# A two-layer attention and long-convolution kernel: the convolution's buffers laid out anew, its inverse table loaded later, the second attention's first weights placed low

## The chip, the cores and the metric

The kernel runs as one program on one core of a Trainium2 chip. The metric is device time in microseconds (us). Before the change three runs took 2643.77, 2644.64 and 2650.95 us; the median is 2644.64 us. One more execution was recorded by the hardware profiler.

The core has a tensor engine (PE, whose weight loads are listed as PEld), a vector engine (DVE), a scalar engine (ACT), GpSimd (POOL) and SyncE (SP), which here only issues DMAs. Each engine works through its own list of instructions in order; an instruction that waits holds up all those behind it on that engine.

## The reference

The input is x of 2048 rows and 640 columns. Two kinds of layer alternate, each twice:

```python
x = x + A(layernorm(x))      # 32-head softmax attention, head size 20, with wqkv and wo
x = x + B(layernorm(x))      # long convolution along the rows, one filter per column
x = x + A(layernorm(x))
x = x + B(layernorm(x))

# A: q, k, v = (x @ wqkv) split in heads; softmax(q k^T / sqrt(20)) v; @ wo
# B: K = 2 * real(sum_n C[d,n] * exp(A[d,n] * dt[d] * l))     # a filter of 2048 taps per column
#    y = irfft(rfft(u, 4096) * rfft(K, 4096), 4096)[:2048] + u * D_skip
```

Everything is float32 at the interface; both A layers share their weights, and both B layers share K, so the filter's spectrum is worked out once.

## The kernel before

The program runs through: first attention (0 to about 1085 us, in which the filter K is also worked out beside the softmax), the first output projection together with the filter's spectrum (to about 1260), the first convolution (to about 1404), the head of the second attention (to about 1469: layer norm, transposes and the projections of the first block of heads), its main part (to about 2447, where ACT computes exponentials nearly without a gap), the second output projection (to about 2498) and the second convolution (to the end).

**Convolution.** Columns are worked in five blocks `b` of 128. `stage1(b, x1, i2)` is the first step of the transform: eight groups `i2`, each a set of 12 matmuls into a PSUM tile `psx` (two such tiles exist), an ACT cast `x10<-psx` to f16 and a DVE subtraction `x11<-psx,x10` for the rest. `stage2a` transposes that (`pst`, copied to `xt` by ACT), `sets(xt)` makes the second step (48 matmuls into `psx`). `product` multiplies with the filter's spectrum: DVE `t<-psx` and `ka<-psx,ka`, then POOL `kb<-t,kb` and `ka<-ka,kb`. `stage3` and `stage4` go back (`psv` with `fa`, then `psy` with the inverse table `eb`, 2048 KB), and DVE adds `psy` to x. These steps are staggered over a loop `n`: step `n` has the transposes of column part `n`, the product of part `n-4`, and `psy` from `n = 14` on.

The spectrum lies in DRAM in `kha` and `khb`, one tensor each, stored by ten pairs of DMAs (`kha<-kn`, `khb<-kn`). `factors` loads one piece of 256 KB of each per step; there are five buffers `ka` and three `kb`, so a load `kb` is issued when POOL has used the one three steps earlier. `eb` is loaded whole before the first `stage1`, in memory that overlaps the tiles `u` and `kn` of the stage before.

**Second attention's head.** `stage(...)` loads a weight and returns a function that later splits it in f16 halves: ACT casts (`wb`, in the trace `wb<-b0s`), DVE subtracts (`wb<-b0s,wb`), and in the second attention a DVE maximum `wm<-b0s` looks for the largest weight. `b0s` and `b1s` (320 KB each) hold the first q and k weights. They lie in memory that overlaps `eb`, so that they are loaded after the last `psy` of the first convolution. Four row groups `i4` are normalised (`bn_stats`, `va`, `lt`, `rs`, `nb`, then ACT `xn`), transposed (`pst`), split in `xh` (ACT) and `xl` (DVE), and multiplied (`pq`, `pv`).

The order on each engine comes from the order of the code, changed by a scheduler: an instruction goes onto its engine's list when the scheduler's model finds its inputs and its memory free, so a buffer's address also sets the place in the list.

In the listing below, line numbers are those of the profile. A helper issues most DVE, ACT and DMA instructions and is L78 in all rows; matmuls of the convolution are L1430, its transposes L1452, POOL's products L1480; the transposes of attention's head are L823, its `pq` L773.

Of the kernel before, what the change touches and what calls it, by code (L numbers as in the profile page):

```python
# [21 lines left out]
P = 128  # L22
# [4 lines left out]
H = 32  # L27
# [60 lines left out]
def mha_s4d_kernel(ctx, tc, x_in, wqkv, wo, lar, aim, cr, ci, ldt, dsk,  # L88
# [26 lines left out]
    kd = dram.tile([D, L], F32, name="kd")  # L115
    dtd = dram.tile([1, D], F32, name="dtd")
    wd = dram.tile([P, 3, len(LV), D], F32, name="wd")
    kha = dram.tile([2 * NCT, P, 4, 4, P], F32, name="kha")
    khb = dram.tile([2 * NCT, P, 4, 4, P], F32, name="khb")
    qs = dram.tile([2, D, L], F16, name="qs")  # L120
    ks = dram.tile([2, D, L], F16, name="ks")
    qm = dram.tile([H, L], F16, name="qm")
# [309 lines left out]
    def attention(x, stats):  # L432
# [50 lines left out]
        def stage(c0, n, tag, dst=None, pool=None):  # L483

            full = QW if pool or tag == "v" else P
            ts = tag + "s" if pool else "ws"
            wt = (pool or q2).tile([P, NCT, QW], F32, tag=ts, bufs=1, name=ts)[:, :, :n]
            cols = c0 if isinstance(c0, tuple) else (c0,)
            m = n // len(cols)
            for k, c_ in enumerate(cols):  # L490
                sy.dma_start(wt[:, :, k * m:k * m + m], wqkv[:, c_:c_ + m].rearrange("(t p) c -> p t c", p=P))

            def make():
                bufs = 1 if tag == "v" else 2
                wh, wl = dst or [q2.tile([P, NCT, full], F16, tag=tag + t, bufs=bufs, name=tag + t)[:, :, :n]
                                 for t in "hl"]
                if not first_layer:
                    ve.reduce_max(wm[:, made[0]:made[0] + 1], wt, axis=AX.XY,
                                  apply_absolute_value=True)
                made[0] += 1  # L500
                if pool:
                    se.activation(wh, wt, AF.Copy, scale=WS)
                else:
                    ve.tensor_scalar_mul(wh, wt, WS)
                ve.scalar_tensor_tensor(wl, wt, WS, wh, ALU.mult, ALU.subtract)
                return wh, wl
            return make
        made = [0]

        def post(w_, b, tq, qc, pool=None):  # L510

# [245 lines left out]
        with ExitStack() as c2:  # L757
            psum(c2, M=2, S=4)
            hp = c2.enter_context(tc.tile_pool(name="hp", bufs=1))
            xp = c2.enter_context(tc.tile_pool(name="xnp", bufs=2))  # L760
            self_ = hp.tile([P, NBLK * H], F32, name="self")
            NQ = 3 if first_layer else 1
            wv = [hp.tile([P, NCT, NQ * QW], F16, name=f"wv{n}") for n in range(2)]
            wb = [[hp.tile([P, NCT, P], F16, name=f"wb{w_}{n}") for n in range(2)] for w_ in range(2)]
            last[0] = None

            def block0(tq):
# [23 lines left out]
                return ts  # L791

            coming = load_x(0)
            made_ = [stage(n * D, P, f"b{n}", wb[n], hp) for n in range(2)]
            if first_layer:
                filler[:2] = kgen(), False
                weave(1)
            sy.dma_start(self_, c_sel)
            for i4 in range(4):
                xr = coming  # L800
                if i4 < 3:
                    coming = load_x(i4 + 1)
                if stats is None:
                    mv, rs = ln_stats(lambda i: xr[i], 4)
                else:
                    mv, rs = stats(i4)
                xn = []
# [12 lines left out]
                for ct in range(NCT):  # L820
                    pt = pst("S", [P, 512], F32, tag="S", name="pst")
                    for i in range(4):
                        te.transpose(pt[:, i * P:i * P + P], xn[i][:, ct * P:ct * P + P], ident)  # L823
                    sl = slice(512 * i4, 512 * i4 + 512)
                    se.copy(xh[:, ct, sl], pt)
                    ve.tensor_sub(xl[:, ct, sl], pt, xh[:, ct, sl])
                block0(i4)
                if i4 == 0:
                    for make in made_:
                        make()  # L830
                    nxt.append(stage((P, D + P), 64, "w"))
                else:
                    values4(i4 - 1)
# [561 lines left out]
    def ssm(x, uh, ul, consts, last):  # L1395
        st = None
        if not last:
# [4 lines left out]
            mv = sp_.tile([P, NI, 2], F32, name="mv5")  # L1402
            done = {}

            def final(i4):

                if i4 not in done:
                    s4 = slice(4 * i4, 4 * i4 + 4)
                    for i in range(4 * i4, 4 * i4 + 4):
                        ve.bn_stats(st[:, i, NCT - 1, :], x[:, i, (NCT - 1) * P:])  # L1410
                        ve.bn_aggr(mv[:, i, :], st[:, i, :, :])
                    done[i4] = mv[:, s4, :], rstd(mv[:, s4, :], 4, sp_, f"rs{i4}")
                return done[i4]
        e1, f2, id16, fa = consts
        with ExitStack() as c:
            c1 = c.enter_context(tc.tile_pool(name="s1", bufs=1))
            if last:
                cx = c.enter_context(tc.tile_pool(name="sx", bufs=2))
            c4 = c.enter_context(tc.tile_pool(name="s4", bufs=1))
            c2 = c.enter_context(tc.tile_pool(name="s2", bufs=2))  # L1420
            c3 = c.enter_context(tc.tile_pool(name="s3", bufs=3))
            if not last:
                cx = c2
            order = {}

            def at(name, made):
# [1 line left out]

            def mm(*a, **k):
                at("pe", te.matmul(*a, **k))  # L1430
            eb = c1.tile([P, NI, 2, P], F32, name="eb")
            sy.dma_start(eb, c_eb.rearrange("p (i r k) -> p i r k", i=NI, r=2))

            def stage1(b, x1, i2):
                bs = slice(b * P, b * P + P)
# [78 lines left out]
            def new_x1():  # L1514
                return [cx.tile([P, 4, NI // 2, 4, 32], F16, name=f"x1{k}") for k in range(2)]

            x1 = new_x1()
            for i2 in range(8):
                stage1(0, x1, i2)()
            ks, t1s, vs = {}, {}, {}  # L1520
            NQ = 8 * NCT
            nxt, px = None, None
            sums = None
            for n in range(NQ + 15):
# [3 lines left out]
                if n < NQ:  # L1528
                    if q == 0 and b:
                        x1 = nxt  # L1530
                    if n % 4 == 0:
                        xt = c4.tile([P, 2, 4, 4, P], F16, name="xt")
                    stage2a(x1, q, xt)
                if 2 <= n < NQ + 2:
                    ks[n - 2] = factors(*divmod(n - 2, 4))
                if sums:
                    sums[0]()
                if 4 <= n < NQ + 4:
# [7 lines left out]
                    sums = None  # L1546
                if 6 <= n < NQ + 6:
                    m, ch = divmod(n - 6, 4)
                    if m % 2 == 0 and ch == 0:
                        vs[m // 2] = c2.tile([P, 2, NI, 4, 32], F32, name="v")  # L1550
                    stage3(vs[m // 2], m % 2, ch, t1s.pop(n - 6))
                if 14 <= n < NQ + 14:
                    bb, i2 = divmod(n - 14, 8)
# [240 lines left out]
```

## Time and profile before

| quantity | value |
|---|---|
| runs | 2643.77, 2644.64, 2650.95 us (median 2644.64) |
| profiled execution: span from the first to the last instruction | 2647.0 us |
| busy in that span: PE, PEld, DVE, ACT, POOL | 2492.4, 1409.8, 1519.5, 2344.0, 801.7 us |
| mean granted TensorE clock | 0.994 of full speed |
| chain of work that ended last: ACT, PE, issue, DVE, DMA, POOL | 59, 20, 10, 3, 2, 1 % |

Busy shares are over the whole span, and the stages have different limits: in the main part of both attentions ACT is busy nearly throughout, in the convolutions PE and POOL share the load. What a change in one stage is worth has to be read in that stage: which engine ends last there, and what released it. The profiled execution's span is the only time that the profile has for it; it is 2.4 us above the median of the runs.

### The profile page before, as it was taken

The numbers are of one execution on the slowest core, as the hardware profiler recorded it, in microseconds if no ns is written. First come the engines' busy times: TensorE is split into PE (matmuls) and PEld (weight loads), VectorE is DVE, ScalarE is ACT, GpSimd is POOL, SyncE is SP. The second block draws the span as 40 slices with busy tenths as digits, with TensorE's granted clock in tenths as the row PEclk, the third lists the DMA queues.
The fourth block names the chain that finished last, engine by engine and source line by source line (L and its number), as shares of the span: only waits on it lengthen the run. The fifth ranks groups of instructions, "written<-read, shape, count | busy, mean of one in ns | idle before, by whom it ended". The sixth has DMA issues, their size and how long they took to land.

```text
span 2647.0 us, 118800 instructions
## 1 busy us (share of the span) xinstructions
PE 2492.4 (94%) x52388; PEld 1409.8 (53%) x52388; DVE 1519.5 (57%) x3430; ACT 2344.0 (89%) x2763; POOL 801.7 (30%) x1230
## 2 busy tenths in 40 slices
PE   6899999999999999899898999999999998999898
PEld 3444444454444444587896544454444443444898
DVE  7587777777765887577786323232232222143875
ACT  7899999999999999655665899999999999999574
POOL 1123333233323332111681122222222223222285
PEclk9999999999999999999999999999999999999999
DMA  6522222322222221654652111121121113222466
GB/s 206 189 53 77 68 74 62 82 65 63 61 54 59 53 63 38 234 206 163 213 173 64 47 53 50 51 60 45 45 66 39 50 34 87 71 66 61 137 190 184
DMA packets 188158, 241.99 MB, mean 91 GB/s; under 512 B 43504, under 2 KB 128816, under 8 KB 186224
## 3 DMA queue, kind: packets, MB, share of 16 engines
q1 hardware_dynamic: 151936, 188.28, 22.6%
q0 software_dynamic: 35696, 46.01, 7.4%
q8 instruction: 413, 6.77, 1.1%
q14 instruction: 113, 0.93, 0.1%
HBM read 158.16 MB, written 76.00 MB: 88 GB/s over the span
## 4 chain that ended last, share of the span: by engine, by line
ACT 59%; PE 20%; issue 10%; DVE 3%; DMA 2%; POOL 1%; SPq 0%; ACTq 0%; POOLq 0%; DVEq 0%
ACT pt L78 57%; PE psy L1430 3%; PE pa L903 2%; PE psv L1430 2%; PE po L193 2%; PE psx L1430 2%; PE S L868 2%; PE pst L1452 1%; PE pkx L193 1%; PE pv L586 1%; PE m L620 1%; PE pkt L196 1%; PE pq L773 1%; DMA kb<-khb 1%; DMA kop<-ks 1%
## 5 line engine op out<-in xcount | busy, mean ns | idle before, releaser
L78 ACT ACTIVATE pt<-S 128x1024 f32<-128x1024 f32 x2048 | 1927.7, 1033 | 27.9 <-PE S L868 15.5
L903 PE MATMUL pa<-pt,V 64*32 64x512 f32 x16384 | 1096.9, 589 | 1.4 <-DVE oc L78 1.4
L868 PE MATMUL S<-qop,kop 61*32 61x512 f16 x16384 | 877.2, 380 | 82.7 <-ACT pt L78 67.8
L868 PEld LDWEIGHTS <-kop 61*32 61x32 f16 x16384 | 366.9, 89 | 737.3 <-issue 619.2
L903 PEld LDWEIGHTS pa<-pt,V 64*32 64x32 f32 x16384 | 312.7, 106 | 72.0 <-issue 8.6
L78 POOL DMA_DIRECT2D dn<-oc x248 | 122.7, 501 | 574.2 <-DVE oc L78 574.1
L78 DVE TENSOR_SCALAR qc<-m 128x512 f32<-128x512 f32 (+1 forms) x68 | 46.8, 688 | 312.0 <-PE m L620 312.0
L78 POOL DMA_DIRECT2D db<-dn x248 | 125.4, 512 | 141.5 <-DMA dn<-dr 136.9
L78 POOL DMA_DIRECT2D ot<-oc x256 | 130.5, 517 | 88.4 <-DVE oc L78 55.5
L620 PE MATMUL m<-xl,wh 64*32 64x512 f16 x2560 | 143.8, 376 | 0.3 <-issue 0.3
L620 PE MATMUL m<-xh,wh 64*32 64x512 f16 x2560 | 144.1, 378 | 0.0
L620 PE MATMUL m<-xh,wl 64*32 64x512 f16 x2560 | 143.8, 377 | 0.0
L78 DVE COPY oc<-pa 128x512 f32<-128x512 f32 x64 | 44.2, 690 | 172.9 <-PE pa L903 168.9
L78 ACT COPY xt<-pst 128x1024 f16<-128x1024 f16 x80 | 81.3, 1016 | 60.8 <-PE pst L1452 60.8
L620 PEld LDWEIGHTS <-wh 64*32 64x32 f16 x5120 | 90.3, 93 | 73.3 <-issue 30.8
L78 POOL DMA_DIRECT2D dn<-dr x62 | 34.6, 558 | 287.3 <-DVE dr L78 248.6
L1480 POOL TENSOR_TENSOR kb<-t,kb 128x512 f32<-128x512 f32 x76 | 97.2, 1280 | 65.2 <-DVE t L78 40.8
L78 DVE TENSOR_SCALAR V<-m 128x160 f32<-128x160 f32 x64 | 20.7, 324 | 163.4 <-PE m L586 163.4
L78 DVE TENSOR_TENSOR kb<-ktab 128x512 f32<-128x512 f32 x160 | 106.2, 683 | 0.0
L586 PEld LDWEIGHTS <-xh 128*128 128x128 f16 x960 | 79.7, 98 | 46.7 <-issue 31.4
L1480 POOL TENSOR_TENSOR ka<-ka,kb 128x512 f32<-128x512 f32 x76 | 97.5, 1283 | 6.0
L337 PEld LDWEIGHTS m<-kb,ka 128*32 128x32 f32 x3840 | 60.8, 109 | 71.0 <-issue 52.4
(312 smaller groups left out, 3936.4 us busy)
## 6 DMA issues: line engine op xcount, KB each, us to landing
ka<-kha SPq DMA_DIRECT2D x80, 256.0 KB
kb<-khb SPq DMA_DIRECT2D x80, 256.0 KB
db<-dn POOLq DMA_DIRECT2D x248, 64.0 KB, 3.2
kop<-ks SPq DMA_DIRECT2D x176, 80.0 KB
kpw<-wd POOLq DMA_DIRECT2D x60, 192.0 KB, 3.9
qop<-qs SPq DMA_DIRECT2D x256, 40.0 KB
ot<-oc POOLq DMA_DIRECT2D x256, 40.0 KB, 3.0
kha<-kn SPq DMA_DIRECT2D x20, 512.0 KB
```

What stands on the lines that cost most here:

```text
L78: made = f(out, *a, **k)
L193: chain(te.matmul(*a, **k))
L196: chain(te.transpose(*a, **k))
L337: chain(te.matmul(ps[32 * j:32 * j + 32, c8, :], a[n][:, ch, :], b[n][:, dd, :], start=(n == 0), stop=(n == 2), tile_position=(0, 32 * j)))
L586: chain(te.matmul(ps[:, :n], a_[:, ct, sl], m[:, ct, :], start=(k == 0), stop=(k == 14)))
L620: chain(te.matmul(ps[r][32 * t:32 * t + 32, :], a_[rows, ct, 32 * u:32 * u + 32], m[rows, ct, 512 * v:512 * v + 512], start=(k == 0), stop ...
L773: te.matmul(pq, a_[:, ct, :], m[:, ct, sl], start=(n == 0), stop=(n == 14))
L868: chain(te.matmul(S[32 * t:32 * t + 32, 512 * r:512 * r + 512], kt_[rows, kc + 32 * t:kc + 32 * t + 32], qt[rows, :], start=True, stop=Tru ...
L903: chain(te.matmul(pa[r][32 * j:32 * j + 32, :], V[rows, kt, VP * h:VP * h + 32], pts[j // 2][rows, 512 * (j % 2):512 * (j % 2) + 512], sta ...
L1430: at("pe", te.matmul(*a, **k))
L1452: at("pe", te.transpose(pt[:, k, g, :], of_group(x1[k], 4 * q + g), id16))
L1480: at("pool", getattr(ge, f)(*a))
```

## The change

1. `kha` and `khb` become ten DRAM tiles each. A load waits for the stores of its own tile and not for all of them, and the first loads are issued before the last store.
2. The convolution's memory pools are laid out anew. The two buffers `v` become `va` and `vb` in separate pools. `eb` shares a pool with `va`, is allocated and loaded at step `n = 6`, behind the loads of part 4; the factors of parts 0 to 2 are issued ahead of `stage1`. `x1` (the tiles of `x10`, `x11`) lies at 72416 to 105184 of the second convolution's memory, where it lay at 51936 to 84704.
3. In the attention's head the tiles of `b0s`, `b1s` are allocated first, so they lie at 65440 to 71840 (before 74528 to 80928), below the memory of `eb`. The looks for the largest value of these two are put off until the last `xl` of row group 0, and so are the statistics of row groups 2 and 3.

```diff
-    kha = dram.tile([2 * NCT, P, 4, 4, P], F32, name="kha")
-    khb = dram.tile([2 * NCT, P, 4, 4, P], F32, name="khb")
+    kha, khb = ([dram.tile([P, 4, 4, P], F32, name=f"kh{t}{m}") for m in range(2 * NCT)] for t in "ab")
...
-                    ve.reduce_max(wm[:, made[0]:made[0] + 1], wt, axis=AX.XY,
-                                  apply_absolute_value=True)
+                    look = lambda n=made[0]: ve.reduce_max(wm[:, n:n + 1], wt, axis=AX.XY, apply_absolute_value=True)
+                    looks.append(look) if made[0] < 2 else look()
...
-            self_ = hp.tile([P, NBLK * H], F32, name="self")
-            wv = [hp.tile([P, NCT, NQ * QW], F16, name=f"wv{n}") for n in range(2)]
-            wb = [[hp.tile([P, NCT, P], F16, name=f"wb{w_}{n}") for n in range(2)] for w_ in range(2)]
...
+            wb = [[], []]
             made_ = [stage(n * D, P, f"b{n}", wb[n], hp) for n in range(2)]
+            for w_ in range(2):
+                wb[w_].extend(hp.tile([P, NCT, P], F16, name=f"wb{w_}{n}") for n in range(2))
...
-                    mv, rs = stats(i4)
+                    mv, rs = stats(i4, turned if i4 > 1 else None)
...
+                if i4 == 0:
+                    turned = xl_.ins
+                    for look in looks:
+                        tie(look(), turned)
...
-                        ve.bn_stats(st[:, i, NCT - 1, :], x[:, i, (NCT - 1) * P:])
+                        tie(ve.bn_stats(st[:, i, NCT - 1, :], x[:, i, (NCT - 1) * P:]), after)
...
+            c0, c4 = (c.enter_context(tc.tile_pool(name=n, bufs=1)) for n in ("s0v", "s4"))
+            cx = c.enter_context(tc.tile_pool(name="sx", bufs=2))
+            c3 = c.enter_context(tc.tile_pool(name="s3", bufs=3))
             c1 = c.enter_context(tc.tile_pool(name="s1", bufs=1))
-            if last:
-                cx = c.enter_context(tc.tile_pool(name="sx", bufs=2))
-            c4 = c.enter_context(tc.tile_pool(name="s4", bufs=1))
-            c2 = c.enter_context(tc.tile_pool(name="s2", bufs=2))
-            c3 = c.enter_context(tc.tile_pool(name="s3", bufs=3))
-            if not last:
-                cx = c2
...
-            eb = c1.tile([P, NI, 2, P], F32, name="eb")
-            sy.dma_start(eb, c_eb.rearrange("p (i r k) -> p i r k", i=NI, r=2))
...
+            ks = {k: factors(*divmod(k, 4)) for k in range(3)}
...
-                if 2 <= n < NQ + 2:
+                if 5 <= n < NQ + 2:
                     ks[n - 2] = factors(*divmod(n - 2, 4))
+                if n == 6:
+                    vs[0] = c1.tile([P, 2, NI, 4, 32], F32, name="va")
+                    eb = c1.tile([P, NI, 2, P], F32, name="eb")
+                    at("sp", sy.dma_start(eb, c_eb.rearrange("p (i r k) -> p i r k", i=NI, r=2)))
```

The first place is SP at the start of the first convolution. Before, `eb` stands behind the last store and ahead of every load; `ka`, `kb` are loads of the spectrum, in order of the part.

```order
734 L78 DMA khb<-kn_28866 128x1024
735 L78 DMA khb<-kn_28870 128x1024
736 L78 DMA eb<-in_c_eb 128x4096
737 L78 DMA ka<-kha 128x512
738 L78 DMA kb<-khb 128x512
739 L78 DMA ka<-kha 128x512
```

In the changed kernel the same stretch of SP reads as follows; `kha_66` is the first of the ten tiles, `kha_67` the second.

```order
735 L78 DMA ka<-kha_66 128x512
736 L78 DMA khb_85<-kn_28888 128x1024
737 L78 DMA kb<-khb_76 128x512
...
744 L78 DMA ka<-kha_67 128x512
745 L78 DMA kb<-khb_77 128x512
746 L78 DMA eb<-in_c_eb 128x4096
747 L78 DMA ka<-kha_67 128x512
748 L78 DMA kb<-khb_77 128x512
```

`eb` has moved behind five pairs of loads (parts 0 to 4) and stands ahead of the loads of part 5. The second convolution has the same order.

The second place is ACT at the start of the second convolution: `x<-psx` are the casts of `stage1`, `oh<-otl`, `u` and `uhx` belong to the second output projection. Before:

```order
431 L78 CAST oh<-otl 128x640
432 L78 CAST x_55485<-psx_55487 128x4x4x32
433 L78 CAST oh<-otl 128x640
434 L78 CAST x_55485<-psx_55502 128x4x4x32
435 L78 ACT_TABLE_LOAD
...
457 L78 CAST uhx<-u 128x640
458 L78 CAST x_55485<-psx_55517 128x4x4x32
459 L78 ACTIVATE lt<-va 128x1
460 L78 CAST x_55485<-psx_55532 128x4x4x32
```

In the changed kernel, where the numbers after `x_` and `psx_` are only names of buffers:

```order
432 L78 CAST oh<-otl 128x640 x2
433 L78 ACT_TABLE_LOAD
...
453 L78 CAST uhx<-u 128x640
454 L78 CAST x_55517<-psx_55519 128x4x4x32
455 L78 CAST x_55517<-psx_55534 128x4x4x32
456 L78 ACTIVATE lt<-va 128x1
457 L78 CAST x_55517<-psx_55549 128x4x4x32
458 L78 CAST x_55517<-psx_55564 128x4x4x32
459 L78 CAST x_55517<-psx_55579 128x4x4x32
460 L78 ACTIVATE u<-x,nb,rs 128x640
```

The first two of the eight casts have moved from the beginning of the output projection to its end, behind the last `uhx` but one. DVE's first two subtractions have moved with them.

The third place is DVE at the end of the first convolution and the start of the second attention's head. Before, the weights stand behind all the statistics:

```order
2235 L78 BN_AGGR mv_28890<-st_28889 128x2 x2
2236 L78 TENSOR_REDUCE wm<-b0s 128x1
2237 L78 TENSOR_SCALAR va<-mv_28890 128x4
2238 L78 TENSOR_REDUCE wm<-b1s 128x1
2239 L78 SCALAR_TENSOR_TENSOR wb_31480<-b0s,wb_31479 128x640
2240 L78 SCALAR_TENSOR_TENSOR wb_31482<-b1s,wb_31481 128x640
2241 L78 CAST sel<-self 128x192
2242 L78 TENSOR_TENSOR xl<-pst,xh 128x512 x5
2243 L78 TENSOR_REDUCE wm<-b0s 128x1
```

In the changed kernel:

```order
2199 L78 SCALAR_TENSOR_TENSOR wb_31503<-b0s,wb_31502 128x640
2200 L78 TENSOR_TENSOR x<-x,psy 128x2x128
2201 L78 RECIPROCAL rs<-lt 128x4
2202 L78 TENSOR_TENSOR x<-x,psy 128x2x128
2203 L78 TENSOR_TENSOR lt<-rs 128x4
2204 L78 SCALAR_TENSOR_TENSOR wb_31505<-b1s,wb_31504 128x640
...
2228 L78 TENSOR_TENSOR xl<-pst,xh 128x512 x5
2229 L78 TENSOR_REDUCE wm<-b0s 128x1
2230 L78 TENSOR_REDUCE wm<-b1s 128x1
2231 L78 SCALAR_TENSOR_TENSOR nb<-mv_28908,rs 128x4
```

The two `wb` subtractions stand among the last additions of `psy`, the two looks `wm` behind the five `xl`. On ACT the casts `wb<-b0s`, `wb<-b1s` have moved in the same way, ahead of the first `lt` and of the four `xn`; on SP the loads of `b0s` and `b1s` wait for the first of the last nine groups of `psy` where they waited for the last.

## Rows read from the trace of the kernel before

**Rows 1.** The page's first line: span and instructions.

```profile
span 2647.0 us, 118800 instructions
```

**Rows 2.** Busy time by stretch: us, PE, PEld, DVE, ACT, POOL, clock, DMA share, GB/s.

```profile
1260.00:1404.00 144.00, 134.22 (x1900) 126.69 (x1897) 113.11 (x303) 87.35 (x166) 102.00 (x90) 0.99 0.54 172
2498.00:2647.00 149.00, 133.72 (x1872) 126.22 (x1871) 98.64 (x213) 86.41 (x162) 98.14 (x77) 0.97 0.63 187
```

**Rows 3.** Chain of work that ended last, first convolution's start: start us, us, what.

```profile
1260.73 4.64 DMA khb<-kn
...
1267.82 8.42 DMA kb<-khb
```

**Rows 4.** Timeline of ACT and PE there; in brackets idle time before, and its releaser.

```profile
1275.16 1.01 ACT L78 COPY xt<-pst 128x1024 f16<-128x1024 f16 x1 [0.25 <-PE pst L1452]
1276.23 0.91 PE L1430 MATMUL psx<-xt,f2s 32*32 32x512 f16 x48 [0.43 <-DMA kb<-khb]
```

**Rows 5.** Timeline of SP's DMA issues: the loads kb of parts 4 and 5.

```profile
1283.58 0.32 SPq L78 DMA_DIRECT2D kb<-khb  x1
...
1286.15 0.32 SPq L78 DMA_DIRECT2D kb<-khb  x1
```

**Rows 6.** Busy time by stretch while eb and the first loads move (columns as above).

```profile
1274.00:1278.00 4.00, 3.09 (x83) 2.67 (x83) 2.23 (x6) 2.53 (x5) 0.00 (x0) 1.00 0.96 351
```

**Rows 7.** Chain at part 5's load, and POOL's addition that takes it.

```profile
1286.15 5.19 DMA kb<-khb
...
1291.48 1.30 POOL L1480 TENSOR_TENSOR kb<-t,kb 128x512 f32<-128x512 f32 x1
```

**Rows 8.** Second convolution's stage1: casts as a group, then timeline of ACT, PE, DVE.

```profile
L78 ACT CAST x<-psx x8: 567/580/587, 2460.7 to 2505.3; 128x512 f16<-128x512 f32 x8
...
2498.55 0.58 ACT L78 CAST x<-psx 128x512 f16<-128x512 f32 x1
2499.91 0.27 PE L1430 MATMUL psx<-uhx,e1s 128*128 128x128 f16 x1 [4.91 <-DVE x L78]
2503.92 0.83 DVE L78 TENSOR_TENSOR ulx<-u,uhx 128x640 f16<-128x640 f32 x1
2505.28 0.59 ACT L78 CAST x<-psx 128x512 f16<-128x512 f32 x1 [0.47 <-PE psx L1430]
```

**Rows 9.** First convolution's last psy on PE, and SP's issue of b0s.

```profile
1395.35 8.43 PE L1430 MATMUL psy<-v,eb 128*128 128x128 f32 x72
1403.81 0.38 SPq L78 DMA_DIRECT2D b0s<-in_wqkv  x1
```

**Rows 10.** Timeline of ACT in the second attention's head.

```profile
1400.30 0.20 ACT L78 ACTIVATE lt<-va 128x4 f32<-128x4 f32 x1 [4.10 <-DVE va L78]
...
1403.95 3.36 ACT L78 ACTIVATE xn<-x,nb,rs 128x640 f32<-128x640 f32 x4 [0.27 <-PE psy L1430]
...
1409.06 2.03 ACT L78 CAST xh<-pst 128x512 f16<-128x512 f32 x4
```

**Rows 11.** Timeline of DVE in the second attention's head.

```profile
1407.29 0.82 DVE L78 TENSOR_REDUCE wm<-b0s 128x1 f32<-128x640 f32 x1 [0.46 <-DMA b0s<-in_wqkv]
1408.42 0.82 DVE L78 TENSOR_REDUCE wm<-b1s 128x1 f32<-128x640 f32 x1 [0.23 <-DMA b1s<-in_wqkv]
1409.15 0.81 DVE L78 SCALAR_TENSOR_TENSOR wb<-b0s,wb 128x640 f16<-128x640 f32 x1
...
1410.79 3.13 DVE L78 TENSOR_TENSOR xl<-pst,xh 128x512 f16<-128x512 f32 x5
```

**Rows 12.** PE's fifth transpose group there, its clock, and pq on the chain.

```profile
1411.53 0.66 PE L823 MATMUL pst<-ident,xn 128*128 128x128 f32 x4 [3.51 <-DVE xl L78]
1412.00:1414.00 2.00, 2.00 (x8) 0.67 (x7) 2.00 (x5) 1.64 (x3) 0.00 (x0) 0.60 0.45 142
1412.18 8.26 PE pq L773 x30
...
1436.94 6.47 PE pq L773 x30
```

More of the change, by code (lines that the diff above doesn't have):

```diff
@@ L507, in stage @@
             return make
-        made = [0]
+        made, looks = [0], []
         def post(w_, b, tq, qc, pool=None):
@@ L793, in attention @@
             coming = load_x(0)
+            wb = [[], []]
             made_ = [stage(n * D, P, f"b{n}", wb[n], hp) for n in range(2)]
+            for w_ in range(2):
+                wb[w_].extend(hp.tile([P, NCT, P], F16, name=f"wb{w_}{n}") for n in range(2))
+            self_ = hp.tile([P, NBLK * H], F32, name="self")
+            wv = [hp.tile([P, NCT, NQ * QW], F16, name=f"wv{n}") for n in range(2)]
             if first_layer:
@@ L825, in attention @@
                     se.copy(xh[:, ct, sl], pt)
-                    ve.tensor_sub(xl[:, ct, sl], pt, xh[:, ct, sl])
+                    xl_ = ve.tensor_sub(xl[:, ct, sl], pt, xh[:, ct, sl])
+                if i4 == 0:
+                    turned = xl_.ins
+                    for look in looks:
+                        tie(look(), turned)
                 block0(i4)
@@ L1403, in ssm, with final @@
             done = {}
-            def final(i4):
+            def final(i4, after=None):
                 if i4 not in done:
@@ L1515, in new_x1 @@
                 return [cx.tile([P, 4, NI // 2, 4, 32], F16, name=f"x1{k}") for k in range(2)]
+            NQ = 8 * NCT
+            t1s, vs = {}, {}
+            ks = {k: factors(*divmod(k, 4)) for k in range(3)}
             x1 = new_x1()
@@ L1519, in ssm @@
                 stage1(0, x1, i2)()
-            ks, t1s, vs = {}, {}, {}
-            NQ = 8 * NCT
             nxt, px = None, None
@@ L1531, in ssm @@
                     if n % 4 == 0:
-                        xt = c4.tile([P, 2, 4, 4, P], F16, name="xt")
+                        xt = c0.tile([P, 2, 4, 4, P], F16, name="xt")
                     stage2a(x1, q, xt)
-                if 2 <= n < NQ + 2:
+                if 5 <= n < NQ + 2:
                     ks[n - 2] = factors(*divmod(n - 2, 4))
+                if n == 6:
+                    vs[0] = c1.tile([P, 2, NI, 4, 32], F32, name="va")
+                    eb = c1.tile([P, NI, 2, P], F32, name="eb")
+                    at("sp", sy.dma_start(eb, c_eb.rearrange("p (i r k) -> p i r k", i=NI, r=2)))
                 if sums:
@@ L1548, in ssm @@
                     m, ch = divmod(n - 6, 4)
-                    if m % 2 == 0 and ch == 0:
-                        vs[m // 2] = c2.tile([P, 2, NI, 4, 32], F32, name="v")
+                    if m % 2 == 0 and ch == 0 and m:
+                        pool, name = ((c1, "va"), (c0, "vb"))[m // 2 % 2]
+                        vs[m // 2] = pool.tile([P, 2, NI, 4, 32], F32, name=name)
                     stage3(vs[m // 2], m % 2, ch, t1s.pop(n - 6))
```

## The prediction

> **What bounds the kernel now.** I read the page's first line first [rows 1], then the busy time by stretch, since the change touches only two convolutions and the 65 us between the first of them and the second attention's softmax. In both convolutions PE is busy 93 and 90% of the stretch and POOL 71 and 66% [rows 2]: neither is idle enough for DMA to be the general limit, so I looked at each end of them for the wait that is last. The chain of waits names two DMA pieces at the first convolution's start, a store of 4.64 us and a load of 8.42 us [rows 3]. The reader is to test these against the timeline: the first `sets` matmul starts at 1276.23, the ACT copy `xt` that it reads ends at 1275.16 + 1.01 = 1276.17 [rows 4]. It follows the copy by 0.06 us. The load that the chain names landed at the same moment, and POOL needs it only two us later. So that start is bound by the transform's own steps, and a DMA that ends earlier changes nothing there.
>
> **The change, part by part.** All times are against the profiled span of 2647.0 us, which lies 2.4 us above the median of the runs; I add the sum to the median.
>
> *Ten tiles, and loads ahead of the last store.* They remove the 4.64 us store and the 2048 KB of `eb` from in front of the first loads. By the paragraph above this is worth nothing: the cover is `stage1`, the transposes and `xt`, which end at 1276.17 anyway. Bounds: a gain of 0.43 us (PE's idle time that the row puts down to the load [rows 4]) and 0. I take 0.
>
> *`eb` late.* It is issued right behind the load `kb` of part 4, so at about 1283.58 + 0.4 = 1284.0 [rows 5], in front of `ka` and `kb` of part 5. Without it, `kb` of part 5 was issued at 1286.15 and landed 5.19 us later at 1291.34, and POOL's addition began at 1291.48 [rows 7]: there is 0.1 us of slack. With it, SP's queue holds at 1284.0 the rest of `kb` of part 4 (up to 0.26 MB), `eb` (2.10 MB) and the two loads of part 5 (0.52 MB), 2.6 to 2.9 MB. At the 351 GB/s that the same transfers reached with the DMA engines 96% busy [rows 6] this is 7.5 to 8.2 us, until 1291.5 to 1292.2; the way from the last byte to the start of the waiting instruction comes on top, and I allow up to 2 us for it. So part 5 lands 0.1 to 2.9 us late; I take 1.5, the middle, as no row is nearer to one end. DVE's multiplication by `ka` waits too, and behind it on DVE the subtractions `x` of `stage1`, which PE waits for. POOL runs without a gap there, so a lost us is not won back. If the transfer is slower than that, the price goes up to the whole transfer, 2.10 MB / 351 GB/s = 6.0 us. Part 6 has two steps more and catches up. The second convolution has the same order and the same pace, so again 1.5. Together +3.0, between 0.2 and 5.8.
>
> The Trainium skill ("DMA: Bandwidth & Descriptors", section "Queues, rings and completion order") says that all DMAs issued by SP share one row of rings and that each ring's descriptors are consumed in order; by that rule a small load behind `eb` waits for nearly all of it, which is what the sum assumes. If the queue let the small loads pass, this term would be near 0 and the sum 3.0 lower. The trace before has no large transfer ahead of a needed load, so no row shows which.
>
> *`stage1` of the second convolution.* Before, the first cast runs at 2460.7, in the output projection, and only six of the eight are left at 2498.55 [rows 8]. Now `x10`, `x11` lie where the second attention's tiles and the projection's `otl` lay, and all eight casts stand behind `uhx` at 2498.55. PE had also worked ahead by two groups; its next `psx` (group 4) waited 4.91 us for DVE to free a tile and started at 2499.91 [rows 8]. Now the same matmul slot does group 2. Two steps more at the pace of the rows, (2505.28 - 2499.91) / 4 = 1.3 us from group 4's matmuls to group 7's cast, are 2.7 us. A check from another side: the last `u` now stands behind the cast of group 4, which comes two steps later, so `u`, `uhx` and DVE's `ulx` (2503.92, 0.83 [rows 8]), which group 7 needs, are later by about the same. After that nothing differs, so the delay goes to the end. Bounds: 0.6 + 0.6 for two casts alone at the row's 0.58, and 3.6 with a late `ulx`. I take +2.8. What the output projection wins by the two casts that leave it is nothing, because PE's projection matmuls run without them.
>
> *The second attention's head.* Before, `b0s` was issued at 1403.81, after the last of nine `psy` groups [rows 9], and landed by 1407.29; `b1s` by 1408.42 [rows 11]. Two looks and two subtractions follow on DVE, 4 x 0.82 less overlap, and `xl` starts at 1410.79; PE's fifth transpose group waits 3.51 us for it [rows 11, 12]. Now the issue waits for the first of the nine, 1395.35 + 8.43 / 9 = 1396.3, so the weights land about 7.5 us earlier, near 1399.8 and 1400.9. The looks leave the path. But the casts of both weights now stand ahead of `lt` on ACT: `lt` ran at 1400.30 [rows 10], now it waits for `b1s` and a cast, about 1401.65, so 1.35 later. From there to `xn` DVE has two subtractions `wb` more (0.81 each [rows 11]) and a few statistics less; `xn` also loses its wait of 0.27 for the last `psy`. I put `xn` at 1404.75, 0.8 late. The last `xn` ends 3.36 later, at 1408.1, its transposes at 1408.8, `xh` starts at 1408.9 (before 1409.06 [rows 10], where it stood behind the casts), and `xl` 0.6 later at 1409.5 instead of 1410.79. So PE's wait ends 1.3 us earlier. Against this, `wv`, whose load needs the buffer of `b0s`, now waits for a look that comes after `xl`, and group 1's `nb` stands behind both looks: some of it comes back, 0.3. I take -1.0. Bounds: -5.3, if all 3.51 us of PE's wait go and PE keeps its clock. Its clock was granted 0.60 in 1412 to 1414, after that wait, and the first `pq` pair took 8.26 us where the next took 6.47 [rows 12], 1.79 more. The other bound is +1, if the late `wv` holds PE.
>
> Sum: 0 + 3.0 + 2.8 - 1.0 = +4.8 us. On the median that is 2644.64 + 4.8 = 2649.4 us; the profiled span would be about 2651.8.
>
> **Rivals.**
>
> *Late loads wait for the whole table (slower).* Place: SP's queue at part 5 of both convolutions. Price: not 1.5 but 6.0 each, if `eb` holds the queue alone and parts 5 and 6 both miss their step. For it: 0.1 us of slack, and POOL without a gap. Against it: at 351 GB/s the queue would be empty by 1292.2. Time: 2644.64 + 12.0 + 2.8 - 1.0 = 2658.4. It decides the sign beyond 0.3% when each stall is over 3.1.
>
> *The head gives all that it can.* The full 5.3. For it: the looks, 1.6 us, were on the path without need. Against it: `lt` behind the casts. Time: 2644.64 + 3.0 + 2.8 - 5.3 = 2645.1.
>
> *The chain is right about the first convolution's start (faster).* If the first products did wait for store and loads, 4.64 us and 6.0 us of `eb` go: 2649.4 - 10.6 = 2638.8; with half of the head's gain 2636.6. For it: the two pieces of the chain [rows 3]. Against it: `xt` ends 0.06 us before the matmul [rows 4].
>
> **How the numbers follow.** A run can tell no change from a change only beyond about 0.3%, 7.9 us: faster is below 2636.7, slower above 2652.6. The forecast has a chance of 0.52, with its own range of 2645.5 to 2653; the table's whole wait 0.16; the head's full gain 0.20; the chain's reading 0.12. Half of the chain's case would be below 2636.7, and a little of the head's: faster 0.08. Slower is nearly all of the first rival and a tenth of the forecast: 0.20. Same is 0.72. The range that leaves 2 in 10 out is 2640 to 2656.
>
> **What would show it.** In the trace after: `eb` issued near 1284 in the first convolution, and a gap on POOL before the addition of part 5, put down to DMA, 0 to 3 us, and one like it in the second. All eight casts of the second `stage1` behind 2498, and the first `xt` some 2.8 us later after the output projection's end than before. `b0s` issued seven us before the last `psy` ends, `lt` behind two casts, PE's wait before the fifth transpose group near 2 us. I am wrong if the first `sets` matmul starts earlier relative to the last spectrum store by more than 1 us, if POOL shows no gap at part 5, or if the time is below 2640.

## The result, and the profile after

The changed kernel takes 2658.69 us (median of 6 runs, 2657.26 to 2662.37); the kernel before, on the same chip, 2648.05 (6 runs, 2643.77 to 2652.91). The ratio is 1.0049, interval 1.004 to 1.0059, which is 13.0 us (10.6 to 15.6): slower by 0.4 to 0.6%. The medians differ by 10.6 us, the lower end of that. The forecast was 2649.4, with a range up to 2656. The first rival, "late loads wait for the whole table", gave 2658.4.

The page's first line, which answers to [rows 1]:

```profile
span 2656.9 us, 118785 instructions
```

Runs of one kernel scatter by some us, and part of that arises before the changed stages, so I compare stretches inside the two profiled runs. Each begins and ends with the start of an instruction that both traces show; the last ends with the span.

| stretch | before | after | difference | forecast |
|---|---|---|---|---|
| program start to the first `sets` matmul | 1276.2 | 1272.8 | -3.5 | 0 |
| first `sets` to first `psy` of the first convolution | 28.2 | 34.7 | +6.5 | +1.5 |
| first `psy` to the second attention's first exponential | 164.8 | 162.6 | -2.2 | -1.0 |
| first to last exponential | 979.5 | 979.4 | -0.1 | 0 |
| last exponential to POOL's first product of the second convolution | 66.3 | 69.4 | +3.1 | +2.8 |
| that product to the end | 131.9 | 138.0 | +6.1 | +1.5 |

The four stretches of the change give +13.5 us, from one profiled execution of each kernel; that lies inside the ratio's interval (0.0049 x 2648 = 13.0), above the difference of the medians. The -3.5 of the first is scatter: it was there some 1150 us earlier, at the first attention's first exponential (114.4 after, 117.8 before).

**First convolution.** The timeline of PE, then of SP, POOL and DVE, and one piece of the chain of waits (start us, us, what; in brackets idle time before, and its releaser). They answer to [rows 4, 5, 7].

```profile
1272.76 0.91 PE L1431 MATMUL psx<-xt,f2s 32*32 32x512 f16 x48 [0.43 <-ACT xt L78]
...
1293.60 0.27 PE L1431 MATMUL psx<-uh,e1s 128*128 128x128 f16 x1 [4.79 <-DVE x L78]
...
1307.49 1.06 PE L1431 MATMUL psy<-va,eb 128*128 128x128 f32 x8
```

```profile
1280.11 0.32 SPq L78 DMA_DIRECT2D kb<-khb  x1
1280.47 0.43 SPq L78 DMA_DIRECT2D eb<-in_c_eb  x1
1280.95 0.43 SPq L78 DMA_DIRECT2D ka<-kha  x1
```

```profile
1286.73 1.27 POOL L1479 TENSOR_TENSOR kb<-t,kb 128x512 f32<-128x512 f32 x1 [1.49 <-DMA kb<-khb]
...
1293.06 1.26 POOL L1479 TENSOR_TENSOR kb<-t,kb 128x512 f32<-128x512 f32 x1 [3.69 <-DVE ka L78]
```

```profile
1292.26 0.69 DVE L78 TENSOR_TENSOR ka<-psx,ka 128x512 f32<-128x512 f32 x1 [3.42 <-DMA ka<-kha]
```

```profile
1280.95 11.29 DMA ka<-kha
```

The load `ka` of part 5, issued right behind `eb`, takes 11.29 us where `kb` of part 5 took 5.19 before [rows 7]; the load that comes last is now `ka`. DVE stands 3.42 us for it, POOL behind DVE 3.69. The load `kb` of part 4, issued 0.36 us before `eb`, is late too, by 1.49. POOL's two gaps are 5.2 us together, and PE's next `psx` stands 4.79 us for DVE's `x`, which comes behind that `ka`. The view by stretch (columns as in [rows 2]) shows the transfer, and what the wait did to PE:

```profile
1280.00:1284.00 4.00, 3.31 (x76) 2.66 (x76) 2.68 (x8) 1.87 (x4) 3.84 (x5) 1.00 0.88 207
1284.00:1288.00 4.00, 3.73 (x50) 3.61 (x49) 1.93 (x3) 3.65 (x6) 2.51 (x2) 1.00 0.94 379
1288.00:1292.00 4.00, 0.81 (x11) 0.69 (x11) 0.79 (x2) 1.56 (x3) 1.29 (x2) 0.96 0.94 352
1292.00:1296.00 4.00, 2.40 (x17) 2.40 (x17) 2.90 (x6) 0.58 (x1) 2.86 (x3) 0.50 0.48 176
```

In 1280 to 1292 the DMA engines moved 4 x (0.207 + 0.379 + 0.352) = 3.75 MB. PE, busy for 0.81 of the four us to 1292, then works at a granted clock of 0.50, the 1.2 GHz level, to 1296 and on to 1298. That is the likely rest between the 5.2 us of the gaps and the 6.5 of the stretch, though no run isolates it: POOL has two more gaps there, this one of 0.66 us and one of 0.21 three us later, put down to DVE's `t`, which reads PE's `psx`.

```profile
1301.51 1.27 POOL L1479 TENSOR_TENSOR kb<-t,kb 128x512 f32<-128x512 f32 x1 [0.66 <-DVE t L78]
```

**Second convolution.** POOL at parts 4 and 5 there: the same two gaps, 4.6 us together.

```profile
2530.42 1.27 POOL L1479 TENSOR_TENSOR kb<-t,kb 128x512 f32<-128x512 f32 x1 [0.92 <-DMA kb<-khb]
...
2536.72 1.26 POOL L1479 TENSOR_TENSOR kb<-t,kb 128x512 f32<-128x512 f32 x1 [3.66 <-DVE ka L78]
```

Its `stage1` on ACT, which answers to [rows 8]: first two casts, last cast, and the first `xt`, which was at 2507.15 before.

```profile
2499.02 1.06 ACT L78 CAST x<-psx 128x512 f16<-128x512 f32 x2
...
2508.29 0.58 ACT L78 CAST x<-psx 128x512 f16<-128x512 f32 x1 [0.90 <-PE psx L1431]
2510.20 1.01 ACT L78 COPY xt<-pst 128x1024 f16<-128x1024 f16 x1 [1.33 <-PE pst L1451]
```

**The second attention's head.** SP, then ACT, then PE; they answer to [rows 9, 10, 12].

```profile
1399.60 0.38 SPq L78 DMA_DIRECT2D b0s<-in_wqkv  x1
```

```profile
1403.47 0.74 ACT L78 ACTIVATE wb<-b0s 128x640 f16<-128x640 f32 x1 [4.15 <-DMA b0s<-in_wqkv]
...
1405.05 0.19 ACT L78 ACTIVATE lt<-va 128x4 f32<-128x4 f32 x1
1408.12 3.36 ACT L78 ACTIVATE xn<-x,nb,rs 128x640 f32<-128x640 f32 x4 [2.88 <-issue]
```

```profile
1405.45 2.94 PE L1431 MATMUL psy<-va,eb 128*128 128x128 f32 x24 [1.26 <-DVE x L78]
1409.09 0.65 PE L824 MATMUL pst<-ident,xn 128*128 128x128 f32 x4 [0.70 <-DVE sel L78]
...
1411.53 0.66 PE L824 MATMUL pst<-ident,xn 128*128 128x128 f32 x4 [0.16 <-ACT xn L78]
1413.26 0.66 PE L824 MATMUL pst<-ident,xn 128*128 128x128 f32 x4 [1.07 <-DVE xl L78]
```

```profile
1412.00:1414.00 2.00, 0.93 (x7) 0.58 (x6) 1.92 (x6) 2.00 (x5) 0.00 (x0) 1.00 0.54 150
1414.00:1416.00 2.00, 2.00 (x10) 0.87 (x9) 2.00 (x4) 0.54 (x1) 0.00 (x0) 1.00 0.00 0
```

PE waits 1.07 us for `xl` where it waited 3.51, and its clock stays at 1.00 where 1412 to 1414 had 0.60 [rows 12]. The subtractions `wb` on DVE delay the last additions, and PE's last `psy` stand 1.26 us. That is not on the way to the transposes: `psy` ends at 1408.39, PE then stands 0.70 us more, and its transposes follow `xn`, which starts at 1408.12.

### The profile page after: what moved, and what is told of

Read it like the earlier page. It is cut to its first block, busy times and chain, and to the rows that moved or that the text cites. A ratio compares the mean times of both kernels' runs of the same rounds, so it can differ in the third digit from the quotient of the medians.

```text
span 2656.9 us, 118785 instructions
## 1 busy us (share of the span) xinstructions
PE 2493.6 (94%) x52388; PEld 1409.7 (53%) x52388; DVE 1519.3 (57%) x3430; ACT 2343.4 (88%) x2763; POOL 799.4 (30%) x1230
## 4 chain that ended last, share of the span: by engine, by line
ACT 60%; PE 16%; issue 11%; DMA 4%; DVE 3%; POOL 1%; SPq 0%; ACTq 0%; POOLq 0%; DVEq 0%
ACT pt L78 58%; PE po L192 2%; PE psv L1431 2%; PE psy L1431 2%; PE psx L1431 2%; PE pa L908 1%; PE pst L1451 1%; PE S L873 1%; DMA ka<-kha 1%; DMA otl<-ot 1%; PE pkx L192 1%; PE pkt L195 1%; DMA kop<-ks 1%; PE pkf L192 1%; PE pq L769 1%
```

## The experiments

"Gaps" are POOL's at parts 4 and 5, in run 5 at parts 3 and 4. The kernel before, measured beside the runs, took 2646.88 us (27 runs) for runs 1 to 4, 2646.87 (21) for runs 5 to 7 and 2646.60 (12) for runs 8 and 9; the ratios are against these.

**1. The table first again.** Everything else of the change stays.

```diff
             ks = {k: factors(*divmod(k, 4)) for k in range(3)}
+            vs[0] = c1.tile([P, 2, NI, 4, 32], F32, name="va")
+            eb = c1.tile([P, NI, 2, P], F32, name="eb")
+            at("sp", sy.dma_start(eb, ...))
...
-                if n == 6:
-                    vs[0] = ...; eb = ...; at("sp", sy.dma_start(eb, ...))
```

> The changed kernel with one thing moved: eb is allocated and loaded right behind the loads of parts 0 to 2, ahead of stage1, in both convolutions. Theory 1 (the late table holds up the loads of parts 4 and 5): no gap on POOL at parts 4 and 5, about 6 us less in each convolution, 2646.5 us. Rival (the loss lies in the new addresses or the ten tiles): within 2 us of the changed kernel, 2658.7.

Measured: 2648.92 us (2644.69 to 2653.02, 10 runs), ratio 1.0008, interval 0.9999 to 1.0018. POOL at parts 4 and 5:

```profile
1285.56 1.30 POOL L1479 TENSOR_TENSOR kb<-t,kb 128x512 f32<-128x512 f32 x1
...
1288.17 1.29 POOL L1479 TENSOR_TENSOR kb<-t,kb 128x512 f32<-128x512 f32 x1
```

No gap. First `sets` to first `psy` takes 28.1 us, the second convolution's rest 133.9. Against the changed kernel that is 6.6 and 4.1 us less: the late issue of `eb` is about 11 us of the 13. The rest is still 2.0 over the kernel before (runs 3 and 4 have 132.8 and 132.3). That is one late load near the end, in run 1 and then in the kernel before:

```profile
2617.98 1.27 POOL L1479 TENSOR_TENSOR kb<-t,kb 128x512 f32<-128x512 f32 x1 [2.55 <-DMA kb<-khb]
```

```profile
2618.19 1.28 POOL L1480 TENSOR_TENSOR kb<-t,kb 128x512 f32<-128x512 f32 x1 [0.56 <-DMA kb<-khb]
```

The waits differ by 2.0 us. Why this load, issued long after the table has landed, takes longer in run 1 is not shown. The ten tiles and the early loads bring nothing: 28.1 against 28.2.

**2. `x1` low again** in the second convolution: at 60128 to 92896, where it lay at 51936 before the change and lies at 72416 in the changed kernel. The pool `s4` changes places with it.

```diff
-            c0, c4 = (c.enter_context(tc.tile_pool(name=n, bufs=1)) for n in ("s0v", "s4"))
-            cx = c.enter_context(tc.tile_pool(name="sx", bufs=2))
+            c0 = c.enter_context(tc.tile_pool(name="s0v", bufs=1))
+            if last:
+                cx = c.enter_context(tc.tile_pool(name="sx", bufs=2))
+            c4 = c.enter_context(tc.tile_pool(name="s4", bufs=1))
+            if not last:
+                cx = c.enter_context(tc.tile_pool(name="sx", bufs=2))
```

> The changed kernel with the pool of x1 placed ahead of ka and t2 in the second convolution, so that x10 and x11 lie at 60128 to 92896. Theory 1 (the address moved two casts behind the projection, and these cost 2.6 to 3.4 us): both casts run near 2460 again, the first xt is 2.6 us earlier after the last uhx but one, 2655.5 us. Rival (another step sets the start of the second convolution, the two casts were hidden): less than 1 us, 2658.

Measured: 2655.53 us (2650.05 to 2660.79, 6 runs), ratio 1.0033, interval 1.0018 to 1.0048. The first two casts are back in the output projection, and PE's next group is that of [rows 8] again, with the same wait:

```profile
2499.26 0.27 PE L1435 MATMUL psx<-uhx,e1s 128*128 128x128 f16 x1 [4.91 <-DVE x L78]
```

Last exponential to first product: 66.4 us, as before the change. The gaps stay (4.5 us in the first convolution, 3.75 in the second). So the late `stage1` is worth 3 us, by the place of `x1` (with that of `s4`).

**3. Both.** The edits of 1 and 2 together.

> Both edits: eb loaded behind parts 0 to 2, and x1 at 60128 to 92896 in the second convolution. Theory 1 (the terms add; what is left of the change is the head's gain of 2.4 us): 2643.5 us, or 2 to 3 us less than the kernel before, which ran at 2648 here. Rival (the terms hide each other): 2646 or more, no difference from before.

Measured: 2645.31 us (2642.61 to 2651.72, 10 runs), ratio 0.9995, interval 0.9985 to 1.0004. The stretches are 28.0, 163.1, 66.4 and 132.8 us: the two losses are gone, and of the head's gain 1.7 us are left, less than the total can tell from nothing.

**4. The table in eight pieces** of 256 KB, one in each of the steps 6 to 13.

```diff
-                    at("sp", sy.dma_start(eb, ...))
+                if 6 <= n < 14:
+                    at("sp", sy.dma_start(eb[:, 2 * n - 12:2 * n - 10], ...[:, 2 * n - 12:2 * n - 10]))
```

> The changed kernel with eb loaded in eight pieces of 256 KB, one per step from n = 6 to 13, in place of one load of 2048 KB at n = 6. If the size of the one transfer makes the stall: each step moves 0.79 MB in 2.6 us, 300 GB/s, which is less than the 351 seen, so stalls under 1 us per convolution, 2648 us. If it is the bytes (the engines have no room beside the loads of the steps): the stall is spread over eight steps and about as long, 2656 to 2659 us.

Measured: 2648.49 us (2644.17 to 2652.36, 10 runs), ratio 1.0004, interval 0.9995 to 1.0014. What is left of the gaps in the first convolution, at part 5 and four parts later:

```profile
1289.07 1.28 POOL L1479 TENSOR_TENSOR kb<-t,kb 128x512 f32<-128x512 f32 x1 [0.41 <-DMA kb<-khb]
...
1300.01 1.28 POOL L1479 TENSOR_TENSOR kb<-t,kb 128x512 f32<-128x512 f32 x1 [0.50 <-DVE ka L78]
```

The same bytes, late as well, but spread over eight steps, cost 0.4 us on the first stretch (28.6). It is not lateness that costs, but 2.10 MB in one transfer.

**5. The table on ACT's queue,** so that nothing of SP's stands behind it.

```diff
-                    at("sp", sy.dma_start(eb, ...))
+                    at("act", se.dma_start(eb, ...))
```

> The changed kernel with the one load of eb, at the same step n = 6, issued by ACT in place of SP, so that it does not stand in the queue of the loads ka and kb. If the loads of parts 4 and 5 are late because they stand behind eb in SP's queue: the gaps on POOL shrink from 5.2 us to under 2 us in the first convolution, about 2650 us. If the DMA engines share their bandwidth whatever the queue: gaps as in the changed kernel, 2657 to 2659 us.

Measured: 2659.24 us (2653.31 to 2662.66, 4 runs), ratio 1.0043, interval 1.0027 to 1.0058. Queues in 1276 to 1296 (packets, MB, share of 16 engines), the issue of the table, POOL's gaps, and the load `ka` of part 4 in the second convolution's chain:

```profile
q1 hardware_dynamic: 1243, 2.27, 35.2%
q10 hardware_dynamic: 144, 2.10, 26.1%
```

```profile
1279.37 0.38 ACTq L78 DMA_DIRECT2D eb<-in_c_eb  x1
```

```profile
1286.44 1.27 POOL L1479 TENSOR_TENSOR kb<-t,kb 128x512 f32<-128x512 f32 x1 [1.80 <-DMA kb<-khb]
...
1291.42 1.27 POOL L1479 TENSOR_TENSOR kb<-t,kb 128x512 f32<-128x512 f32 x1 [2.35 <-DVE ka L78]
```

```profile
2523.11 10.98 DMA ka<-kha
```

The edit does more than change the queue. ACT issues the table at the same moment as SP the load `kb` of part 3 (1279.37), one step of 2.6 us earlier among the loads than in the changed kernel, and so the gaps stand at parts 3 and 4, in both convolutions. The stretches are 32.7 and 137.2 us, 2.8 less than in the changed kernel together, which the total of four runs does not show. The load `ka` behind the table, here that of part 4, still takes 10.98 us with no table ahead of it in its queue; that looks as if order in SP's queue had no part in it. The queue rows show a second reading. The table moves in packets of 2.10 MB / 144 = 14.6 KB, the spectrum's loads in packets of 2.27 MB / 1243 = 1.8 KB. If an engine takes a packet from each queue in turn, eight times as many bytes of the table pass in each turn, and the queue of its own is worth little. Runs 8 and 9 were made to tell these apart.

**8 and 9. The table in small packets,** on SP's queue (8) and on ACT's (9). The destination gets 32 bytes of padding after each 2 KB, which keeps the packets at 2 KB. The order of instructions is in run 8 that of the changed kernel and in run 9 that of run 5, with the table one step earlier among the loads.

```diff
-                        mm(py[:, i, :], eb[:, 2 * i2 + i, r, :], ...)
+                        mm(py[:, i, :], eb[:, i2, (2 * i + r) * P:(2 * i + r + 1) * P], ...)
...
-                    eb = c1.tile([P, NI, 2, P], F32, name="eb")
-                    at("sp", sy.dma_start(eb, c_eb.rearrange("p (i r k) -> p i r k", i=NI, r=2)))
+                    eb = c1.tile([P, NI // 2, 4 * P + 8], F32, name="eb")
+                    at("sp", sy.dma_start(eb[:, :, :4 * P], c_eb.rearrange("p (a c) -> p a c", c=4 * P)))
```

> The changed kernel, with one thing altered: the destination of `eb` is padded, so that its one load, at the same place on SP, moves in pieces of 2 KB as the spectrum's loads do, where the changed kernel's 144 packets carry 2.10 MB (about 14.6 KB each). The bytes ahead of part 5 and every instruction's place stay. Theory A (what counts is the bytes that were issued earlier, in order): POOL's gaps at parts 4 and 5 stay at 5.2 us in sum, 2658 us. Theory B (a DMA engine takes turns between loads packet by packet, so that a 14.6 KB packet of the table passes for each 2 KB packet of a spectrum load): with equal packets the spectrum loads get half of the engines, 256 KB land in 5.2 us plus less than 1, gaps under 1 us, about 2649 us. Theory C (turns are taken between queues only, and within SP's queue the order holds): gaps as in the changed kernel, 2658, and the next run alone gains.

> As the run before (the table's load in pieces of 2 KB), but issued by ACT, on a queue of its own. The run with the table on ACT's queue and packets of 14.6 KB had gaps of 1.80 and 2.35 us on POOL and 2659.24 us. Theory A (bytes in order of issue, whatever the queue): the same gaps, 2659. Theories B and C (turns packet by packet between queues): gaps under 1 us in sum, sets to first psy about 28.5 us where the changed kernel had 34.7, about 2649 us.

Measured, 8: 2660.75 us (2657.1 to 2661.42, 4 runs), ratio 1.0047, interval 1.003 to 1.0064. The gap in the first convolution and the load in the second's chain:

```profile
1294.23 1.27 POOL L1479 TENSOR_TENSOR kb<-t,kb 128x512 f32<-128x512 f32 x1 [4.43 <-DVE ka L78]
```

```profile
2527.32 10.76 DMA ka<-kha
```

Measured, 9: 2653.56 us (2646.75 to 2658.72, 9 runs), ratio 1.0024, interval 1.0012 to 1.0036. Queue row of the table (1272 to 1296), the gaps, then in the second convolution the longest load on the chain there, and the load `ka` of part 4, first behind the table, with DVE's instruction that takes it:

```profile
q10 hardware_dynamic: 1040, 2.10, 23.4%
```

```profile
1289.92 1.28 POOL L1479 TENSOR_TENSOR kb<-t,kb 128x512 f32<-128x512 f32 x1 [1.73 <-DMA kb<-khb]
1294.32 1.26 POOL L1479 TENSOR_TENSOR kb<-t,kb 128x512 f32<-128x512 f32 x1 [1.76 <-DMA kb<-khb]
```

```profile
2527.50 6.90 DMA kb<-khb
```

```profile
2525.13 0.44 SPq L78 DMA_DIRECT2D ka<-kha  x1
...
2532.82 0.69 DVE L78 TENSOR_TENSOR ka<-psx,ka 128x512 f32<-128x512 f32 x1 [0.74 <-DMA ka<-kha]
```

Behind the table in one queue a load takes 10.76 us, whatever the packets: theory B falls, and order in the queue does count. Beside it in another queue, with packets of the same size, `ka` of part 4 takes 2532.82 - 2525.13 = 7.7 us (7.6 in the first convolution), where it took 10.98 with the big packets of run 5. That fits turns between queues by packet, which run 5 had hidden. Runs 5 and 9 differ in the packets alone; between 8 and 9 the table also moves one step. But C's "under 1 us" was wrong as well. The engines move some 390 GB/s while the table is under way, the loads get a share of it, and two gaps of 1.7 us remain; the stretches are 31.6 and 134.8 us, where run 8 has 34.3 and 138.3 and the kernel before 28.2 and 131.9. With small packets part 4 in run 8 has no gap in either convolution. That points to the big packets as what made `kb`, issued 0.36 us ahead of the table, late in the changed kernel (1.49 and 0.92 us); but with the same big packets and order run 2 has 0.71 us and, in the second convolution, no gap at part 4, so it is not shown.

**6. The head alone,** its edits made in the kernel before: low weights, late looks, late statistics of row groups 2 and 3 (the third part of the diff of the change).

> The kernel before with the head's part alone: tiles of b0s and b1s first, the looks and the statistics of row groups 2 and 3 put off; convolution as before. Theory 1 (the head gives 2.4 us by itself): 2 to 3 us less from the first psy to the second attention's first exponential (164.8 us before), and 2645.5 us. Rival (it needs the convolution's new layout, because xn's memory overlaps eb): no gain or a loss of up to 1 us, 2647 to 2649 us.

Measured: 2648.44 us (2643.53 to 2650.58, 10 runs), ratio 0.9999, interval 0.999 to 1.0008. First `psy` to first exponential is 164.8 us, as before: nothing gained. PE still waits for `xl`. Its clock is at 0.50 then, but it had fallen before this wait, while the transposes of the four `xn` ran, with PE waits of 1.14 us before the first and 0.16 us between them:

```profile
1406.21 1.12 PE L825 MATMUL pst<-ident,xn 128*128 128x128 f32 x4 [2.32 <-DVE xl L78]
```

```profile
1402.00:1404.00 2.00, 1.85 (x8) 1.10 (x8) 0.55 (x1) 1.63 (x3) 0.00 (x0) 0.59 1.14 255
...
1406.00:1408.00 2.00, 1.78 (x7) 1.18 (x8) 1.97 (x5) 1.92 (x4) 0.00 (x0) 0.50 0.00 0
```

In the old layout `b0s` is still issued at the end of the last `psy` (1399.23 us), and the casts stand behind `xn`. The head's 2 us need the convolution's new layout, where the load is issued ahead of the last 64 `psy`.

**7. The best parts, and the casts of the weights behind `xn`:** run 3, with both casts tied behind the four `xn` of row group 0, so that `lt` and `psy` don't wait for them.

```diff
-                    se.activation(wh, wt, AF.Copy, scale=WS)
+                    tie(se.activation(wh, wt, AF.Copy, scale=WS), behind)
...
-                        make()
+                        make(None if first_layer else normed.ins)
```

> Both edits of e3 (eb behind parts 0 to 2, x1 low), and the casts wb of b0s and b1s held behind the four xn of row group 0, so that lt does not wait for them and DVE's two subtractions leave the additions of psy. If these casts cost the head 1.3 us of PE's psy and delayed xn: first psy to first exponential 160 to 161 us, where e3 has 163.1, and 2643 us, 3 us below the kernel before. If the head is bound by the looks and by what comes after the first pq: 163 us as in e3, 2645.

Measured: 2643.20 us (2638.93 to 2648.63, 11 runs), ratio 0.999, interval 0.9981 to 0.9999: the lowest median of all, and the only one whose interval lies below 1, by a hair. But the head is not where it comes from: it takes 163.9 us, more than run 3's 163.1. `psy` is no longer held, yet PE then waits longer for `xl`, and the clock falls again:

```profile
1391.86 7.53 PE L1435 MATMUL psy<-va,eb 128*128 128x128 f32 x64
...
1404.62 0.66 PE L824 MATMUL pst<-ident,xn 128*128 128x128 f32 x4 [2.17 <-DVE xl L78]
```

```profile
1404.00:1406.00 2.00, 1.38 (x8) 0.87 (x9) 2.00 (x4) 1.60 (x4) 0.00 (x0) 0.99 0.00 0
1406.00:1408.00 2.00, 2.00 (x7) 0.73 (x5) 2.00 (x4) 0.00 (x0) 0.00 (x0) 0.50 0.00 0
```

The changed stretches of its profiled execution are together 0.3 us shorter than those of the kernel before (28.0, 163.9, 66.5 and 132.5 us), so 3.7 us between the medians are not found there. The intervals of runs 3 and 7 overlap. That run 7 is really faster than run 3, or than the kernel before, stays open.

## Why the prediction was wrong

**The step that failed is the size of "`eb` late".** The mechanism, the place and the sign were right: `eb` was issued at 1280.47, 7.7 us after the first `sets` (forecast 1284.0, 7.8 after), the gap came at part 5 of both convolutions, DVE's `ka` and the subtraction behind it passed it on to PE, nothing of it was won back, and part 6 caught up. The step "So part 5 lands 0.1 to 2.9 us late; I take 1.5, the middle, as no row is nearer to one end" measured 5.1 us at POOL: 1293.06, where the step of [rows 7], shifted by the 3.47 us by which `sets` starts earlier, is 1288.01. Of that 3.42 us are DVE's wait for `ka` of part 5, and 1.49 the gap at part 4. The stretches grew by 6.5 and 6.1 us where the sum had 1.5 each. Three things made it too small.

- *The bytes.* I counted 2.6 to 2.9 MB, what was issued up to the waiting load. The engines moved 3.75 MB from 1280 to 1292. `eb`, the two loads of part 5 and both loads of part 4 are 3.15 MB at most and not enough for that: loads issued behind `ka` of part 5 moved before it had landed. In what order the 16 engines took them I did not follow.
- *The rate.* 351 GB/s came from a stretch in which the table was already moving [rows 6]. The first four us here had 207 GB/s.
- *The second wait and the clock.* The gap of 1.49 us at part 4 was not in the sum, because the load of part 4 is issued ahead of `eb`; in run 8, with 2 KB packets, it is not there. And the stretch is 1.3 us longer than the two gaps; PE's clock at 0.50 after the wait is the likely reason.

I also had the bound at hand. The price "up to the whole transfer", 6.0 us per convolution, is near what was measured (6.5 and 6.1), and as a rival it gave 2658.4. That this meets the 2658.69 so closely is partly luck. The rival wanted parts 5 and 6 both late; part 6 had no gap, and part 4 had one. And both sums start from 2644.64, the median of three runs, where the six runs beside the result have 2648.05 and the 60 beside the experiments 2646.60 to 2646.88: 2 to 3.4 us of the 9.3 by which the forecast missed are that base, the rest is the change. I gave the rival 0.16 since "at 351 GB/s the queue would be empty by 1292.2", which is the same wrong byte count used as evidence against it. That the middle of two ends was taken for want of a nearer row should have gone with a larger chance for the upper end: with 0.1 us of slack, every error of the estimate goes to one side.

The Trainium skill's rule on order in a ring, which the prediction named ("DMA: Bandwidth & Descriptors", section "Queues, rings and completion order"), agrees with these runs as far as queues go: with packets of 2 KB the load takes 10.76 us behind the table and 7.7 beside it. By that rule alone the load `kb` of part 4, issued ahead of the table, would not be late, and it was by 1.49 us. The same section of the Trainium skill says that an engine takes turns between queue rows packet by packet; runs 5 and 9, which differ in the table's packets alone, agree with it (gaps of 4.15 and 3.49 us, 2659.24 and 2653.56), if the profile's packets are the ones that it means.

**`stage1` of the second convolution,** +2.8 forecast, +3.1 measured, and undone by moving `x1` alone (run 2). All eight casts stand behind `uhx`, as forecast. The first `xt` is 3.05 us later (2510.20 against 2507.15), of which 0.6 is the later end of the main part, so `stage1` itself cost 2.4 and not 2.8; another 0.8 us comes between that `xt` and POOL's first product, where the working had nothing. That the sum came so near is in part luck.

**The head,** -1.0 forecast, -2.2 measured. With the 3.0 us by which the first `psy` starts later added, the forecast times were met to 0.4 us: `b0s` issued at 1399.3 (1399.60), `lt` 1404.7 (1405.05), `xn` 1407.8 (1408.12), `xl` 1412.5 (1412.51), the fifth transposes 1413.26 (1413.26), which is the 1.3 us of the forecast. PE comes to its wait at 1412.19, behind transposes that follow the four `xn`, and waits 1.07 us and not about 2. What the sum left out is that its clock then stays at 1.00. I had that only in the bound: up to 1.8 us for the first `pq` pair. -1.3 - 1.8 is -3.1, and that pair does end 3.0 us earlier, counted from the first `psy` (1420.33, before 1420.28); the difference to -2.2, 0.8 us, is given back later, where I had 0.3. That DVE's `wb` hold `psy` for 1.26 us I did not see either; it ends before `xn` lets the transposes run. The rival of -5.3 did not come.

**Ten tiles and early loads,** 0 forecast and 0 measured: the first `sets` again follows `xt` at once, with 0.43 us of idle time as in [rows 4], now put down to `xt`. The rival that believed the chain of waits there is refuted: store and table are gone from in front, and the start has not moved against `xt`.

## What to carry to other kernels

A transfer that is moved out of the way early lands somewhere else: before placing 2 MB in the middle of a pipeline whose loads have 0.1 us of slack, count all bytes that will be in flight until the load that follows is in, those issued behind it too, at the rate of that stretch. If it must be there, cut it in pieces of the size of the loads beside it, one a step; another queue alone does little while its packets are eight times as big. And where a bound is one-sided because nothing is slack, forecast nearer to the bad end.

## What the runs showed of the hardware that was not expected

- A 256 KB load of the spectrum landed in 5.2 us in the kernel before. The first one behind a 2.10 MB load took 11.29 us in the same queue, 10.98 with the large one in another queue in packets of 14.6 KB, and 7.7 with it in another queue in packets of 2 KB.
- A load issued 0.36 us before the large one was late by 1.49 and 0.92 us in the changed kernel, by 0.71 and not at all in run 2; with 2 KB packets (run 8) it was never late.
- In the head of the changed kernel the granted clock stayed at 1.00, the 2.4 GHz level, after PE waits of 1.26, 0.70 and 1.07 us. In run 7 it was at 0.50, the 1.2 GHz level, in the two us after a wait of 2.17 us. In run 6 it had fallen to 0.59 before the wait of 2.32 us, with no wait above 1.14 us shortly before it.
